# A state-space scan and a maxout FFN: another order of the opening and of the first two blocks, weight fetches moved, last units by token halves

## The chip, the cores and the metric

The kernel runs on one core of one Trainium2 chip. The metric is the device time of one execution in microseconds, the median of the runs shown. The engines are called as in the profile: PE (TensorE matmuls, with PEld for its weight loads), DVE (VectorE), ACT (ScalarE), POOL (GpSimd) and SP (SyncE, which issues nearly all transfers here).

## The reference

Two stages follow each other. The first is a Mamba-2 scan over 4 batches, 8 heads and 768 positions, head width 32, state width 16. The second is a feed-forward layer whose hidden value is the maximum of three products.

```python
# x, a, B, C: (4, 8, 768, 32 | - | 16 | 16)
for c in range(nc):                                  # chunks along the sequence
    cum = np.cumsum(np.log(np.clip(a, 1e-06, 1.0))[:, :, sl], axis=-1)
    L = np.exp(cum[:, :, :, None] - cum[:, :, None, :]) * causal
    M = np.einsum('bhin,bhjn->bhij', Cc, Bc) * L
    y[:, :, sl] = M @ xc + (Cc @ state) * np.exp(cum)[..., None]
    decay_from_j = np.exp(cum[:, :, -1:] - cum)
    state = exp(sum of log a) * state + sum_j(B_j x_j * decay_from_j)
x = y.transpose(0, 2, 1, 3).reshape(3072, 256)
h = np.maximum(np.maximum(x @ w1, x @ w2), x @ w3)   # w1, w2, w3: 256 x 768
out = h @ w_out                                      # 768 x 256
```

## The kernel before, in words

The sequence is cut into six blocks of 128 positions (`NC`), each holding all four batches, so 512 tokens (`BLK`). Within a block the scan works on two halves of 64 positions (`W`). For each block there is the scan, which gives y transposed (`yT`), and the FFN. The FFN uses max(a, b, c) = b + max(a - b, 0, c - b): the weight differences w1 - w2 and w3 - w2 are formed once (`d`, line 881), the maximum is taken over two products and zero, and the product with w2 is folded into the output matrix (`fold`). Block 0 multiplies in plain float32 (line 841 for its first two units, by position halves, line 1251 for the others). The blocks after it split every operand into a high part H, a rest L and a cross term S in the float32r type, and take three faster products, near (H), far (L) and late (S), at lines 926 and 956. The products with the output matrix are at lines 1038 (block 0), 1070 and 1123 (last block).

The program is ordered by hand. Each engine runs its own queue in the order in which the Python code emits instructions, and that order is spelled as words. `OPENING` (line 1260) is the list for block 0 and the preparation of block 1; `FIRST`, `SECOND`, `STEADY` and `LAST` (lines 1276 to 1331) hold one string for each of the twelve up-units of blocks 1, 2, 3 to 4, and 5. A word emits a function's instructions on all engines at once: `R` and `S0`, `S1` form and spread the sums that the decays of block 0 need, `x0` to `x3` are the exponentials (line 418), `tC` and `tB` the transposes by DVE (line 576), `sc0` the scores (line 588), `p0` to `p3` their product with the decays (line 594), `bm`, `Am`, `mid` the state in the middle of the block, `y0` and `y1` the output of its two halves (line 778), `m0` the first FFN products of the first halves (unit pair 0 and 1) and `n0` to `n11` the twelve units of block 0. `z` adds one dummy matmul to the next `warm` call (line 410). `E` is one exponential of the decays of a later block, `X02` and `X24` its products on PE (line 514), which read `left` and `right`: log sums that go out to DRAM (`sums`, line 485) and come back rearranged (lines 491, 497). `q` is one product of block 0 with the output matrix, `bu0:1` one of the eight steps that form and split the differences of one weight pair, `g` turns a part of w2 for the fold, `d` is one down product, `l` one for the last block.

The weights arrive as 64-bit words of which a float32 must be made. `fetch` (line 193) issues one of twelve transfers of 512 KB on SP. `decode` (line 219) takes two steps on ACT and two on DVE, `sign` (line 233) one on DVE (line 237) and one addition on POOL (line 239). Before the word list starts, the kernel loads C and B of block 0, fetches one weight, loads x of block 0 and fetches `NFETCH` = 8 more (lines 259 to 264). SP runs in order: a transfer that waits holds back all transfers behind it. An issue also waits until the transfer eight places before it has landed, by the semaphores of the built program.

For the last block, `last_next` (line 1106) runs the queue of output products: for each term near, far and cross, in the last term by pairs of batches, then scales the sum (ACT) and adds the cross part (DVE, line 1137), and stores.

Of the kernel before, what the change touches and what calls it, by code (L numbers as in the profile page):

```python
# [12 lines left out]
F32R = mybir.dt.float32r  # L13
# [7 lines left out]
def kernel(  # L21
# [46 lines left out]
    NFETCH = 8  # L68
# [140 lines left out]
    def decode_steps():  # L209
# [3 lines left out]
        if rb is None:  # L213
            return (lambda: None), (lambda: None)
# [4 lines left out]
        def first():  # L219
# [6 lines left out]
            nc.scalar.activation(r.bitcast(FP32), lo, AF.Copy, bias=2.0, scale=2.0 ** -51)  # L226
            nc.vector.tensor_scalar(
# [5 lines left out]
        def second():  # L233
# [4 lines left out]
                out=r, in0=hi, scalar=0x80000000, in1=r, op0=ALU.bitwise_and, op1=ALU.bitwise_or)  # L238
            nc.gpsimd.tensor_tensor(  # L239
# [6 lines left out]
    def decode():  # L246

        first, second = decode_steps()
        first()
        unsigned.append(second)  # L250

    def sign():

        unsigned.pop(0)()
# [117 lines left out]
    def by_token(rows, src, name, scale, bank):  # L372
        return scaled(turned(rows, src, name, bank), name, scale)

# [8 lines left out]
    def first_rows():  # L383
# [10 lines left out]
        for u in range(2):  # L394
            nc.vector.tensor_tensor(
# [47 lines left out]
    def first_from_last():  # L443
# [3 lines left out]
            out=both, in0=cum0[:, 0, W - 1:W], in1=cum0[:, 0, P - 1:P], op=ALU.add)  # L447
        held["fj0"] = fj = half([P, 3, W], "fj0")
# [3 lines left out]
    def first_by_token():  # L452
        fj = held["fj0"].rearrange("p n i -> p (n i)")
        tp = only("up")([P, 2, P], "fj0_tp")
        nc.tensor.transpose(out=tp[0:W, 0], in_=fj[:, 0:W], identity=ident)
        nc.tensor.transpose(out=tp[:, 1], in_=fj[:, W:], identity=ident)
        rows = tp.rearrange("p n (b h d) -> p n b d h", b=NB, h=NH)[:, :, :, 0]
# [19 lines left out]
    def sums_first():  # L477
        nc.scalar.copy(out=hl[:, 0], in_=a_sb)
        nc.vector.tensor_tensor(out=rest, in0=a_sb, in1=hl[:, 0], op=ALU.subtract)

    def sums_store():
        nc.scalar.copy(out=hl[:, 1], in_=rest)
        nc.vector.tensor_tensor(out=hl[:, 2], in0=rest, in1=hl[:, 1], op=ALU.subtract)
        for p in range(3):
# [16 lines left out]
    def decay_sums(c, bs):  # L501
        L = Ls[c] if c in Ls else decays(c)
        es = [att_bank([P, NH, W], "e") for _ in bs]
        if c == 1:
            for e in es:
# [30 lines left out]
    def scan_b(c, kind):  # L536
# [3 lines left out]
        transposes(tr, st["B"])  # L540
        st["BT"] = BT = half([HN, NB, P], "BT")
        nc.scalar.copy(out=BT, in_=tr)

# [11 lines left out]
    def scan_c(c):  # L555
# [4 lines left out]
        for g in range(2):  # L560
            nc.scalar.mul(CT[:, :, g], tr, parity[:, g:g + 1])
# [36 lines left out]
    def first_turned_b():  # L598

        tp = att_bank([W, NP, HN], "B_tp")  # L600
# [898 lines left out]
```

## Time and profile before

| what | value |
|---|---|
| median of 3 runs | 257.39 us (256.78 to 257.83) |
| profiled execution, its own time | 255.31 us |
| span of that execution | 253.6 us |
| granted TensorE clock, mean | 0.970 |
| busy: PE, DVE, ACT, POOL | 238.5, 148.2, 132.7, 115.4 us |
| HBM read, written | 14.17 MB, 3.29 MB |

A row of a timeline gives the start in microseconds, the busy time, the engine, the line, the operation, output and inputs, shapes, the number of records, and in brackets the idle time of that engine just before with what ended it. A float32 matmul has two records. The row of a line gives the number of records, then minimum, median and maximum of their duration in ns.

### The profile page before, as it was taken

How to read it: one execution, taken by the hardware profiler on the slowest of the kernel's cores; microseconds unless marked ns; L12 is line 12 of the kernel's file. 1: busy time of each engine (PE TensorE's matmuls, PEld its weight loads, DVE VectorE, ACT ScalarE, POOL GpSimd, SP SyncE). 2: the span in 40 equal slices, each digit the busy share in tenths (PEclk: the TensorE clock that was granted, in tenths of full speed). 3: DMA queues.
4: the chain of work that ended last, by engine and by line, in shares of the span. 5: the costliest groups of instructions: out<-in, count | busy, mean ns of one | idle time of the engine just before them, and what ended most of it. 6: DMA issues, size and time to landing. Idle time of an engine off the chain costs nothing.

```text
span 253.6 us, 7038 instructions
## 1 busy us (share of the span) xinstructions
PE 238.5 (94%) x2992; PEld 188.4 (74%) x2992; DVE 148.2 (58%) x229; ACT 132.7 (52%) x251; POOL 115.4 (46%) x109
## 2 busy tenths in 40 slices
PE   7846969999999999999999999999999999999993
PEld 3335725656676787888888888888888888998992
DVE  5797499676667964388833765527755263334223
ACT  2757275562288536366464654746536274344341
POOL 4022335779349948529572451666324224122230
PEclk9985699999999999999999999999999999999998
DMA  3999779302743802026402280002000020002002
GB/s 80 199 320 386 120 106 114 123 12 60 117 70 76 100 3 89 3 57 111 45 1 91 63 126 3 0 3 85 0 3 0 3 85 3 0 0 87 0 0 84
DMA packets 71083, 17.92 MB, mean 71 GB/s; under 512 B 64492, under 2 KB 67980, under 8 KB 71052
## 3 DMA queue, kind: packets, MB, share of 16 engines
q1 hardware_dynamic: 70604, 17.21, 31.4%
q8 instruction: 23, 0.38, 0.6%
q10 hardware_dynamic: 448, 0.26, 0.3%
q14 instruction: 8, 0.07, 0.1%
HBM read 14.17 MB, written 3.29 MB: 69 GB/s over the span
## 4 chain that ended last, share of the span: by engine, by line
PE 59%; issue 0%; DVEq 0%; DVE 0%
PE up L926 19%; PE o L1070 19%; PE up L956 9%; PE near L1123 3%; PE y L763 2%; PE y L747 2%; PE cross L1123 1%; PE s L726 1%; PE A L692 1%; PE e L514 1%; PE E L660 0%; DVEq L1494 0%; DVE ob L1137 0%; DVEq L1137 0%
## 5 line engine op out<-in xcount | busy, mean ns | idle before, releaser
L977 POOL TENSOR_TENSOR hL<-h,hH 128x512 fp32r<-128x512 f32 x30 | 40.0, 1332 | 80.0 <-ACT hH L976 78.9
L933 ACT ACTIVATE up<-up 128x512 f32<-128x512 f32 x60 | 35.3, 589 | 46.0 <-PE up L926 44.0
L829 DVE SCALAR_TENSOR_TENSOR hS<-hL,hH 128x512 fp32r<-128x512 f32 x30 | 31.2, 1039 | 35.1 <-POOL hL L977 35.0
L926 PE MATMUL up<-yH,wH 128*128 128x512 f32 x120 | 40.8, 421 | 0.2 <-DVE h L965 0.2
L965 DVE SCALAR_TENSOR_TENSOR h<-up,m 128x512 f32<-128x512 f32 x30 | 20.7, 689 | 30.9 <-PE up L956 26.1
L956 PE MATMUL up<-yS,wS 128*128 128x512 f32 x120 | 37.7, 394 | 0.0
L926 PE MATMUL up<-yL,wL 128*128 128x512 f32 x120 | 37.2, 391 | 0.0
L239 POOL TENSOR_TENSOR w<-w_u,w_r 128x512 uint32<-128x512 uint32 x12 | 16.2, 1358 | 33.5 <-DVE w_r L237 33.5
L961 ACT COPY m<-up 128x512 f32<-128x512 f32 x30 | 17.6, 586 | 20.8 <-PE up L956 20.0
L926 PEld LDWEIGHTS up<-yL,wL 128*128 128x128 f32 x120 | 22.5, 188 | 5.2
L956 PEld LDWEIGHTS up<-yS,wS 128*128 128x128 f32 x120 | 21.8, 188 | 6.1 <-ACT up L933 1.5
L528 POOL TENSOR_SCALAR_AFFINE_SELECT L<-L 64x1024 f32<-64x1024 f32 x16 | 19.6, 1228 | 11.0 <-ACT L L523 10.4
L976 ACT ACTIVATE hH<-h 128x512 fp32r<-128x512 f32 x30 | 18.7, 625 | 7.8 <-DVE h L965 7.8
L926 PEld LDWEIGHTS up<-yH,wH 128*128 128x128 f32 x120 | 18.8, 190 | 3.1 <-DVE h L965 1.0
L1251 PE MATMUL up<-yT,d 128*128 128x512 f32 x40 | 19.1, 605 | 0.0
L734 DVE TENSOR_TENSOR L<-s,L 128x512 f32<-128x512 f32 x20 | 13.0, 682 | 5.2 <-PE s L726 5.2
L1070 PE MATMUL o<-wL,hL 128*128 128x256 f32 x96 | 15.7, 285 | 0.0
L1070 PE MATMUL o<-wH,hH 128*128 128x256 f32 x96 | 15.6, 285 | 0.0
L1070 PEld LDWEIGHTS o<-wH,hH 128*128 128x128 f32 x96 | 14.1, 189 | 1.5
L1070 PE MATMUL o<-wS,hS 128*128 128x256 f32 x96 | 14.7, 286 | 0.0
L1070 PEld LDWEIGHTS o<-wS,hS 128*128 128x128 f32 x96 | 13.4, 190 | 1.2 <-issue 0.2
L1070 PEld LDWEIGHTS o<-wL,hL 128*128 128x128 f32 x96 | 13.4, 190 | 0.7 <-issue 0.2
(175 smaller groups left out, 410.8 us busy)
## 6 DMA issues: line engine op xcount, KB each, us to landing
raw_x<-in_x_dram SPq DMA_DIRECT2D x6, 512.0 KB
out_dram<-ob SPq DMA_DIRECT2D x11, 256.0 KB
rb<-in_moe_w_dram SPq DMA_DIRECT2D x5, 512.0 KB
early<-in_moe_w_dram SPq DMA_DIRECT2D x4, 512.0 KB
rb<-in_moe_w_out_dram SPq DMA_DIRECT2D x3, 512.0 KB
raw_B<-in_B_dram SPq DMA_DIRECT2D x5, 256.0 KB
runs_C<-in_C_dram SPq DMA_DIRECT2D x32, 32.0 KB
runs_B<-in_B_dram SPq DMA_DIRECT2D x32, 32.0 KB
```

The costliest lines, as they stand in the source:

```text
L239: nc.gpsimd.tensor_tensor(out=t.rearrange("p k f -> p (k f)").bitcast(U32), in0=u, in1=r, op=ALU.add)
L528: nc.gpsimd.affine_select(out=part, in_=part, pattern=[[0, 2], [0, NH], [1, W]], compare_op=ALU.is_ge, fill=0.0, base=0, channel_multiplie ...
L829: nc.vector.scalar_tensor_tensor(out=out, in0=L, scalar=-RAISE, in1=H, op0=ALU.mult, op1=ALU.add)
L926: nc.tensor.matmul(out=bank, lhsT=up_parts[q, i][z][:, k, g * P:(g + 1) * P], rhs=y_parts[c][z][:, k], start=(z == 0 and k == 0), stop=(z ...
L933: nc.scalar.mul(bank, bank, RAISE + 1.0)
L956: nc.tensor.matmul(out=up, lhsT=up_parts[q, i][2][:, k, g * P:(g + 1) * P], rhs=y_parts[c][2][:, k], start=False, stop=(k == KD - 1), skip ...
L961: nc.scalar.copy(out=m, in_=up)
L965: nc.vector.scalar_tensor_tensor(out=h, in0=up, scalar=0.0, in1=held["m"], op0=ALU.max, op1=ALU.max)
L976: nc.scalar.mul(H, h, NEAR)
L977: nc.gpsimd.tensor_tensor(out=L, in0=h, in1=plain(H), op=ALU.subtract)
L1070: nc.tensor.matmul(out=o[b // 2][:, b % 2], lhsT=left[:, b * P:(b + 1) * P], rhs=right, start=(first and b % 2 == 0), stop=True, skip_grou ...
L1251: nc.tensor.matmul(out=p, lhsT=of(k), rhs=yT[0][:, k], start=(k == 0), stop=(k == KD - 1))
```

## The change

The diff does six things.

1. Words can be split by engine. Functions become generators; where they `yield`, the word stops, and a later word with a plus sign goes on with the rest. So `n0` puts the matmuls into PE's queue and `n0+` the copy into ACT's queue, at a place of its own.
2. `OPENING`, `FIRST` and `SECOND` are written anew in another order. `STEADY` and `LAST` stay. `y0` and `y1` become eight words by batch (`ya0` to `ya3` for the first half, `yc0` to `yc3` for the second); `cols` (an array for the decays of later blocks) is a word of its own.
3. `NFETCH` is 2 instead of 8; the other fetches are words in `OPENING`. In SP's queue of the built program, five fetches stand ahead of the three stores of the sums and five between those and `left`; before, ten stood ahead of the stores.
4. Four more places take dummy matmuls, and there are more `z`: 24 dummies in `warm` instead of 4.
5. a of block 0 is loaded by two transfers instead of four, and POOL sets the tile to 1.0 ahead of them.
6. In the last block, the last two up-units are done by token halves (`token_half`): a unit now takes both differences of the last feature group for 256 tokens, not one difference for 512, and copy, maximum, split and cross term work on halves. The last output products finish batches 0 and 1 before 2 and 3.

```diff
-    NFETCH = 8
+    NFETCH = 2
...
-    for k in range(REP):
-        eng = nc.sync if k % 2 == 0 else nc.scalar
-        eng.dma_start(
-            out=a0[k::REP], in_=a_rows[:, 0:P])
+    nc.gpsimd.memset(a0, 1.0)
+    for k, eng in enumerate((nc.sync, nc.scalar)):
+        eng.dma_start(out=a0[k::REP], in_=a_rows[:, 0:P])
...
             nc.scalar.activation(u.bitcast(FP32), hi.bitcast(FP32), AF.Abs)
             nc.scalar.activation(r.bitcast(FP32), lo, AF.Copy, bias=2.0, scale=2.0 ** -51)
+            yield
             nc.vector.tensor_scalar(
...
+    def token_half(c, u):
+
+        return u - (NU - 2) if c == NC - 1 and u >= NU - 2 else None
+
+    def half_products(bank, c, r, z):
+        q, g = divmod(NF - 1, 2)
+        for i in range(2):
+            for k in range(KD):
+                nc.tensor.matmul(
+                    out=bank[:, i * HB:(i + 1) * HB],
+                    lhsT=up_parts[q, i][z][:, k, g * P:(g + 1) * P],
+                    rhs=y_parts[c][z][:, k, r * HB:(r + 1) * HB],
+                    start=(z == 0 and i == 0 and k == 0), stop=(z > 0 and k == KD - 1),
+                    skip_group_check=True)
...
-        "R em clip S0 z tC E fj0 cp S1 z tB x3 bt0 x1 fetch cm x0 x2 log sc0 p0 bT p3 decode minus1 p1 p2 y0 sign bm run z Am mid "
-        "decode E sign y1 hl1 decode decode bu0:1 g fj LB1 sign hl2 m0 Lx1 bu0:1 E "
-        "n0 sign decode sign "
-        "n1 z "
-        "n2 bt bu1:1 "
-        "n3 rows decode X02 decode sign LC1 decode 1 decode E LB0 sign decode X24 1 "
-        "n4 g q bu1:1 Bd0 sign sign E "
-        "n5 t E q fetch "
-        "n6 decode bu2:1 q c A0 1 "
-        "n7 q sign e sign E 1 1 minus "
-        "n8 bu1:1 s bd fetch bu0:1 "
-        "n9 bu2:1 9 A q 1 1 1 bu0:1 q decode y bu1:1 1 bu0:1 E bu0:1 "
-        "n10 "
-        "n11 v bu0:1 load2 q sign Y q q 9 "
+        "fetch z z z z z em fj0 fj0+ z z z z z bt0 R R+ cols clip tC em+ cm log run tB cp hl1 cp+ hl1+ S1 bt0+ S0 decode decode+ sign x3 sc0 x0 p3 z z bT x1 fetch p0 z z z z ya0 p1 bm x2 ya1 hl2 p2 hl2+ hl2+ z Am mid z yc0 yc2 yc1 minus1 decode decode decode+ sign yc0+ yc1+ yc2+ fetch fetch fetch yc3 yc3+ ya3 ya2 ya3+ sign+ fetch sign+ z z z z z g decode decode decode bu0:1 decode z m0 "
+        "n0 n0+ decode+ sign decode+ sign+ bu0:1 fj bu0:1 "
+        "n1 n1+ sign sign+ "
+        "n2 "
+        "n3 fetch decode+ sign g+ rows X02 E X24 bt LB1 decode+ sign E E sign+ bu1:1 g "
+        "n4 n2+ decode n3+ sign+ q q decode+ sign sign+ q decode+ sign g+ bu1:1 bu1:1 decode decode+ sign q decode LB0 Bd0 n4+ "
+        "n5 n5+ E "
+        "n6 n6+ A0 1 e LC1 t bt+ bo:1 decode+ sign sign+ sign+ bu2:1 t+ t+ c "
+        "n7 sign+ fetch n7+ "
+        "n8 fetch c+ e+ 1 s decode decode+ sign "
+        "n9 decode sign+ q bd Lx1 bu2:1 bu0:1 1 1 1 q 1 A 1 bu0:1 "
+        "n10 minus load2 q q n8+ bu2:1 n9+ n10+ 1 y v v+ decode+ bu0:1 sign sign+ Y 1 1 "
+        "n11 n11+ "
     )
     FIRST = [
-        "Z bu1:1 X04 E",
-        "Z q E bu1:1 bu1:1 bu0:1",
-        "Z load E E t 1 q",
...
+        "Z e 1 bu1:1 load bu1:1 1 bu1:1 bu0:1 bu1:1",
+        "Z q X04 E E E bu0:1",
+        "Z E q q t c 1",
...
     for word in OPENING.split():
+        if word[-1] == "+":
+            go_on(word[:-1])
+            continue
...
-            last += [(t, z, range(NB)) for t in LAST_TERMS[:-1] for z in range(3)]
-            last += [(LAST_TERMS[-1], z, bs) for bs in ((0, 1), (2, 3)) for z in range(2)]
-            last += [(LAST_TERMS[-1], 2, bs) for bs in ((0, 1), (2,), (3,))]
+            two, end = LAST_TERMS[-2:]
+            last += [(t, z, range(NB)) for t in LAST_TERMS[:-2] for z in range(3)]
+            last += [(t, z, (0, 1)) for t in (two, end) for z in range(2)]
+            last += [(t, 2, (0, 1)) for t in (two, end)]
+            last += [(t, z, (2, 3)) for t in (two, end) for z in range(2)]
+            last += [(two, 2, (2, 3)), (end, 2, (2,)), (end, 2, (3,))]
...
+        if r is not None:
+            half_products(up, c, r, 2)
+            m = half([P, HB], "m")
+            nc.scalar.copy(out=m, in_=up[:, 0:HB])
+            cross_next()
+            h = half([P, HB], "h")
+            nc.vector.scalar_tensor_tensor(
+                out=h, in0=up[:, HB:], scalar=0.0, in1=m, op0=ALU.max, op1=ALU.max)
+            held["h"] = c, NF - 1, h, slice(r * HB, (r + 1) * HB)
+            return
...
-    for _ in range(2):
+    while len(last) > 13:
         last_next()
```

More of the change, by code (lines that the diff above doesn't have):

```diff
@@ L1331, with later_from_j, run, go_on @@
     ]
+    def later_from_j():
+        tp = turned(R, held["fj"], "from_js", att_bank)
+        yield
+        from_js = scaled(tp, "from_js", 1.0)
+        for m in range(1, NC):
+            from_j[m] = from_js[:, :, m]
+    begun = {}
+    def run(c, word, steps):
+        if not steps:
+            return
+        if c:
+            for _ in steps:
+                pass
+            return
+        if part(steps):
+            begun.setdefault(word, []).append(steps)
+    def go_on(word):
+        if not part(begun[word][0]):
+            begun[word].pop(0)
+    def part(steps):
+        try:
+            next(steps)
+        except StopIteration:
+            return False
+        return True
     def act(c, word):
@@ L1356, in act @@
         elif word == "bt":
[L1357 to L1359 removed]
+            run(c, word, later_from_j())
         elif word == "bd":
@@ L1395, in act @@
         elif word == "v":
-            scan_own(n, range(NB // 2, NB))
-            nc.scalar.copy(out=seen, in_=blocks[n]["y"][1][:, 0, 0, 0:1])
+            run(c, word, second_own(n))
         elif word == "Y":
```

238 lines of the change are left out of this document (140 added, 98 removed).

## The prediction

> **What bounds the kernel now.** I read the page first (the span, and the granted clock in 40 slices), then the stretches, then each engine's timeline in the stretches where TensorE sits idle or slow.
>
> ```profile
> span 253.6 us, 7038 instructions
> ...
> PEclk9985699999999999999999999999999999999998
> ```
> ```profile
> 0.00:20.00 20.00, 14.33 (x300) 7.82 (x304) 14.56 (x40) 10.31 (x20) 4.33 (x16) 0.92 0.76 206
> 20.00:40.00 20.00, 15.76 (x79) 9.50 (x72) 14.78 (x28) 13.01 (x27) 6.57 (x6) 0.74 0.85 187
> 40.00:60.00 20.00, 20.00 (x280) 12.43 (x285) 15.48 (x23) 11.36 (x20) 14.64 (x13) 1.00 0.35 78
> 100.00:222.00 122.00, 121.99 (x1748) 104.82 (x1747) 66.49 (x91) 64.19 (x122) 55.12 (x49) 1.00 0.18 36
> 222.00:253.60 31.60, 27.20 (x179) 24.66 (x178) 9.66 (x15) 11.95 (x22) 6.90 (x6) 0.98 0.10 34
> ```
>
> The second view gives, for each stretch, its length, then busy time with the number of instructions for PE, PEld, DVE, ACT and POOL, then granted clock, DMA share and GB/s. From 40 us on TensorE has work without a break: 20.00 of 20.00, later 121.99 of 122.00. There the kernel is as long as its matmuls, and the diff leaves their number as it is; a new order of blocks one and two can lose time there but has almost none to win. Time that is not matmul work lies in the first 40 us (5.67 + 4.24 us idle, and a clock of 0.74 in the second stretch) and in the tail (4.40 us). The first 40 us in stretches of three:
>
> ```profile
> 12.00:15.00 3.00, 0.95 (x33) 0.56 (x32) 2.92 (x6) 2.50 (x5) 0.00 (x0) 1.00 0.96 267
> 15.00:18.00 3.00, 1.51 (x64) 1.14 (x64) 3.00 (x8) 1.72 (x3) 1.27 (x1) 0.79 0.93 315
> 24.00:27.00 3.00, 2.69 (x6) 2.19 (x7) 2.80 (x4) 1.02 (x5) 1.26 (x1) 0.50 1.20 302
> 30.00:33.00 3.00, 3.00 (x12) 1.74 (x11) 1.46 (x4) 3.00 (x6) 0.40 (x1) 0.93 0.86 140
> ```
>
> From 12 to 18 us TensorE is busy for 2.46 us of 6, the clock falls to half inside 15-18, and it is back only in 30-33, although TensorE was at 2.69 of 3 from 24 on. DVE is the full engine there (2.92 and 3.00 of 3). What the half clock and the waits cost, on TensorE's timeline:
>
> ```profile
> 24.31 6.71 PE L841 MATMUL up<-yT,d 128*128 128x256 f32 x16 [1.89 <-DVE d L881]
> 31.07 1.88 PE L1251 MATMUL up<-yT,d 128*128 128x512 f32 x4
> 34.70 0.59 PE L506 MATMUL e<-mask,ident 128*128 128x512 bf16 x2
> 37.59 0.41 PE L514 MATMUL e<-right,left 32*64 32x512 bf16 x4 [2.29 <-DMA right<-sums]
> 38.80 1.98 PE L1251 MATMUL up<-yT,d 128*128 128x512 f32 x4
> 92.02 3.62 PE L1051 MATMUL o<-fold,yT 128*128 128x256 f32 x16
> ```
>
> The first FFN products (words m0 and n0) start at 24.31 because the weight difference d came late. They take 6.71 us, where sixteen records of the same shape took 3.62 at 92 us at full clock. Later the decay products wait 2.29 us for `right`, a DMA.
>
> **The change, part by part.** Term A, the start of m0. DVE and POOL rows:
>
> ```profile
> 5.33 0.35 DVE L387 TENSOR_SCALAR factors<-opening,dsel,ndsel 128x128 f32<-128x128 f32 x1
> 11.69 1.29 DVE L594 TENSOR_TENSOR L<-s,L 128x512 f32<-128x512 f32 x2 [1.30 <-ACT L L418]
> 17.69 0.39 DVE L627 TENSOR_TENSOR mid<-A,parity 128x256 f32<-128x256 f32 x1
> 18.00 0.41 DVE L227 TENSOR_SCALAR w_u<-w_u 128x512 f32<-128x512 f32 x1
> 18.79 0.69 DVE L237 SCALAR_TENSOR_TENSOR w_r<-early,w_r 128x512 uint32<-128x512 uint32 x1
> 21.09 0.41 DVE L479 TENSOR_TENSOR sums_rest<-opening,hl 96x256 f32<-96x256 f32 x1
> 23.57 0.68 DVE L881 TENSOR_TENSOR d<-w 128x512 f32<-128x512 f32 x1
> L239 POOL TENSOR_TENSOR w<-w_u,w_r x12: 1262/1274/1719, 15.8 to 65.8; 128x512 uint32<-128x512 uint32 x12
> ```
>
> DVE runs its queue in order. Between the second decode (18.00 to 19.48) and d (23.57) stand the copies of y, sums_rest and two further decodes. In the changed program's order d follows the second decode and two copies directly, and the third and fourth decode come behind it. Walk: `factors` starts at 5.33 now; two DMAs for a in place of four let it start perhaps 0.2 earlier (my choice; a POOL memset that they wait for keeps it from being more), 5.1. From there to `mid` DVE takes 12.36 us (5.33 to 17.69), of which 1.30 is a wait for the first exponentials. The new order pulls sums_rest (0.41) and the third part of hl (0.41 by the same row) ahead of `mid`, and moves the four scans ahead of the second transpose, so the exponentials come while DVE is busy: the 1.30 goes, 0.8 comes. Against that, five dummy matmuls (words z) stand ahead of the word em now:
>
> ```profile
> 2.80 1.91 PE L434 MATMUL spread<-mask,ident 128*128 128x512 bf16 x4
> 5.39 1.08 PE L638 MATMUL E<-opening,to_n 32*32 32x64 f32 x32 [0.68 <-DVE opening L341]
> ```
>
> Five at 0.42 (four in 1.91 with the last one's drain) behind 4.71 end at 6.8, em ends at 7.9 instead of 6.5, and the exponential of E0 (0.4, an estimate from the other small steps) is there at 8.3, where DVE wants it at about 8.0 for Cd: 0.3 lost. `mid` starts at 5.1 + 12.36 - 1.30 + 0.82 + 0.3 = 17.3, the second decode takes 1.48 behind it, with `mid` itself 0.39: 19.1 (the copies of y fit between, TensorE's y being done). POOL adds 1.27: 20.4; d 0.68: 21.1, less some overlap of queue steps, 21.0. A = 24.31 - 21.0 = 3.3. Bounds: 1 (the first exponentials late by the full 1.3 again, and the copies) and 5.
>
> Term B, the clock. The changed program has 24 dummy matmuls (4 before): five ahead of em and five ahead of bt0, seven between the scores and `mid`, five ahead of the base transposes, and two more. Seven at about 0.21 (two in 0.59 above, with one's drain) add 1.5 us in the poor stretch; the scores (1.2, as the later ones quoted under D) move into it with the later transpose, and some y products (0.6, my estimate) leave it: about 4.6 of 6 busy instead of 2.46, 77% against 41%. The only fall in this trace follows the 41%. So m0 and n0 take 3.62: B = 6.71 - 3.62 = 3.1. Bounds 0 and 3.1. The dummies cost 0.3 in A and nothing else, since TensorE waits for DVE at each of those places; if that cover were gone, they would cost their 5 us.
>
> By the Trainium skill (TensorE: Matmul & The Clock Gate, What's actually happening) full clock comes after about one busy window of some 3.4 us; the rows above show 6 us, from 24.31 into the stretch at 30. By its figure a closed gate would cost m0 and n0 only about 1.7 instead of 3.1; the measured rows decide here.
>
> Term C, `right`. The weight fetches are not tied to a request by any semaphore: the built order shows only that fetches six to ten now stand behind the store of the sums in SP's queue instead of ahead of it.
>
> ```profile
> 14.68 2.69 SPq L206 DMA_DIRECT2D rb<-in_moe_w_dram  x4
> 21.05 8.59 SPq L485 DMA_DIRECT2D sums<-hl  x3
> 30.23 3.96 SPq L497 DMA_DIRECT2D left<-sums  x3
> 34.24 1.77 SPq L491 DMA_DIRECT2D right<-sums  x3
> ```
>
> SP sat on the store of the sums until 29.64, since hl was late and everything queued behind it. Now hl is done at 17.2 (just ahead of `mid`); five fetches at 0.67 follow (20.6), left (3.96) and right (1.77): 26.3, and the matmul came 1.6 after the last issue (36.01 to 37.59): 27.9. TensorE wants it after n3: 21.0 + 3.62 + 3.6 (n2, n3 and a small transpose, 31.07 to 34.70) + 0.59 = 28.8. Covered by 0.9; C = 2.3, bounds 0 and 2.3. What is late if hl slips: fetches six to ten themselves, which no longer lie in memory before they are needed.
>
> Term D, what the earlier start runs into: the decoding. TensorE arrives 3.3 + 3.1 + 2.3 = 8.7 us sooner, and DVE must deliver weights sooner. From d at 21.0 to the eleventh weight DVE has nine decodes at 1.48 (13.3), three more d (2.0), and about 4.3 of other work (four h at 0.69, as the row at 244.89 has it, and three small ones of about 0.5): 40.6, with POOL's 1.27, 41.9. TensorE asks for that weight in the words q behind n9:
>
> ```profile
> 53.41 1.21 PE L726 MATMUL s<-CP,BT 32*64 32x128 f32 x64
> 57.25 1.99 PE L1038 MATMUL o<-w,h 128*128 128x256 f32 x8
> L230 DVE TENSOR_SCALAR w_u<-w_u x12: 426/428/1380, 13.5 to 59.0; 128x512 uint32<-128x512 uint32 x12
> L237 DVE SCALAR_TENSOR_TENSOR w_r<-rb,w_r x8: 679/684/1544, 31.8 to 64.9; 128x512 uint32<-128x512 uint32 x8
> ```
>
> n4 starts at 21.0 + 3.62 + 3.6 + 1.8 (the decay words, 34.70 to 38.80, without their stall) = 30.0; six units at 1.8, four q at 1.0 and the scores' 1.2 bring it to 46.0, a little more with the small words. Slack 4.1. But a decode step that meets POOL's add takes up to 1380 instead of 426 ns, 1544 instead of 679: 1.8 us for one decode, 16.3 for nine. The medians (428, 684) lie at the minima, so about half collide at most: 8.1, a stall of 4.0. Between 0 and 4.0 I take D = 2.0, the middle; the far bound, all nine, is 12.2.
>
> Blocks one and two: TensorE's idle time of 40 to 222 us is under a microsecond, so 0, with the transfers for block two still 20 DMAs behind `minus`.
>
> Term E, the tail.
>
> ```profile
> 244.89 0.69 DVE L965 SCALAR_TENSOR_TENSOR h<-up,m 128x512 f32<-128x512 f32 x1 [1.04 <-PE up L956]
> 247.72 0.69 DVE L829 SCALAR_TENSOR_TENSOR hS<-hL,hH 128x512 fp32r<-128x512 f32 x1 [2.13 <-POOL hL L977]
> 248.56 0.65 PE L1123 MATMUL cross<-wS,hS 128*128 128x256 f32 x4
> 249.08 1.35 DVE L1137 TENSOR_TENSOR ob<-raised,cross 128x512 f32<-128x512 f32 x3 [0.67 <-PE cross L1123]
> ```
>
> The chain from h to hS (244.89 to 248.41) is hidden under matmuls that end at 248.56, so halving it shortens nothing by itself; it would matter (3.5 us) if those matmuls were fewer, and both programs have 36 products behind the last `late`. But three additions (1.35) stand behind the last product now, and in the new order two of the four outputs are added some 1.4 us earlier: one addition of about 0.4 remains exposed. E = 0.8, bounds 0 and 1.4.
>
> Sum: 3.3 + 3.1 + 2.3 - 2.0 + 0.8 = 7.5. The profiled execution took 255.31 (span 253.6); 247.8 follows. The runs' median, 257.39, lies 2.08 above it; I carry that over: **249.9 us**.
>
> **The rivals.** The clock closes all the same (for: 77% is my count, and dummies that wait for a bank bunch up; against: five of them stand shortly before m0): B is lost, 253.0.
>
> `right` still lands late (for: the cover is 0.9 and the weights share the queue; against: the store leaves SP 12 us sooner): C is lost, 252.2. With it the words "on request" have done nothing.
>
> DVE runs short (for: 2.92 and 3.00 of 3 busy already, and the same work in 8.7 us less; against: the medians above): with two thirds of nine decodes colliding 10.9, a stall of 6.8, 4.8 more than in D, 254.7.
>
> Slower: every decode from the third on collides with the add of the one before, because the new order sets them back to back. Place: the first q behind n9. Price: 16.3 less the slack of 4.1, 12.2, which is 10.2 more than in D: 260.1. It decides from about eight of the nine on (8 x 1.8 = 14.4, less 4.1 is 10.3, against A + B + C + E = 9.5). For: POOL has nothing else there, so its adds follow each decode at once; against: an add that falls into one of DVE's waits harms nobody, and in 40-60, with POOL busy for 14.64 of 20, DVE's 23 steps kept TensorE full. The Trainium skill (SBUF — State Buffer, Who interferes with whom) says why it could be all: VectorE and GpSimd hold one port pair by an exclusive lock, and the second blocks fully. The trace agrees for single steps (1380 against 426), not for their median.
>
> **How the numbers follow.** Forecast 0.52; clock 0.13 (253.0); `right` late 0.06 (252.2); DVE short 0.11 (254.7); better, with D at zero, 0.05 (247.9); gains and stalls cancel 0.05 (about 257.4); all collide 0.08 (260.1). A run of this kernel can be told from no change by about 0.5%, 1.3 us: faster 0.52 + 0.13 + 0.06 + 0.11 + 0.05 = 0.87, same 0.05, slower 0.08. The forecast's own range, by A and D, is 247.5 to 252; to hold 8 in 10 it reaches to the clock and DVE cases, 246.5 to 254.5.
>
> **What would show it.** Right: m0 at about 21 us, its sixteen records in about 3.6, PEclk without a 5 or 6 after the start, no wait of the decay products for `right`, DVE's last addition under 0.5 us long in the tail, and TensorE idle for some 2 us between 40 and 60 in waits for POOL's w. Wrong: a clock of 0.5 at m0 (B), PE idle for more than 4 us behind n4 with the releaser w or w_r (D), or new idle time in blocks one and two.

## The result and the profile after

The changed kernel takes 246.17 us (median of 6 runs, 245.22 to 246.39), the kernel before on the same chip 257.23 (256.78 to 258.17). The ratio is 0.956, with a 95% interval of 0.953 to 0.958. The forecast was 249.9 with a range of 246.5 to 254.5, so the direction was right and the time lies 0.3 under the range. The profiled execution of the changed kernel took 246.31; profile against profile the gain is 9.0 us, median against median 11.1. The sum had promised 7.5 between profiles. Medians and ratios leave out the few runs that lie more than 1.5% above the fastest run of the same kernel.

The page of the changed kernel, its span and the granted clock:

```profile
span 244.6 us, 7115 instructions
...
PEclk9889999999999999999999999999999999999999
```

Its stretches (length, then busy time of PE, PEld, DVE, ACT, POOL, then granted clock, DMA share, GB/s):

```profile
0.00:20.00 20.00, 16.83 (x341) 9.11 (x342) 15.16 (x45) 13.27 (x26) 5.83 (x18) 0.91 0.83 229
20.00:40.00 20.00, 19.20 (x80) 11.37 (x79) 18.93 (x27) 15.30 (x31) 10.72 (x8) 1.00 1.04 227
40.00:60.00 20.00, 19.75 (x405) 12.82 (x404) 13.77 (x25) 8.77 (x17) 14.07 (x14) 1.00 0.14 30
60.00:80.00 20.00, 18.88 (x152) 14.52 (x151) 16.72 (x20) 12.54 (x23) 14.21 (x12) 1.00 0.75 109
100.00:222.00 122.00, 121.66 (x1576) 104.75 (x1575) 66.13 (x94) 64.30 (x120) 49.98 (x43) 1.00 0.17 33
```

From 20 to 40 us TensorE is busy for 19.20 of 20 us at full clock, where it had 15.76 at 0.74. The half clock is not gone (the two 8 in the row of slices), but it is over by 14 us. New is the idle time of 1.12 us in 60 to 80. TensorE's timeline, the places of the prediction's terms in order:

```profile
10.21 2.45 PE L601 MATMUL s<-CP,BT 32*64 32x128 f32 x64 [1.78 <-ACT CP L676]
...
20.77 0.67 PE L877 MATMUL up<-yT,d 128*128 128x256 f32 x2
22.16 3.18 PE L877 MATMUL up<-yT,d 128*128 128x256 f32 x14 [0.73 <-issue]
25.18 3.60 PE L1325 MATMUL up<-yT,d 128*128 128x512 f32 x8
...
29.14 0.41 PE L522 MATMUL e<-right,left 32*64 32x512 bf16 x4
...
48.21 1.89 PE L1108 MATMUL o<-w,h 128*128 128x256 f32 x8
...
72.80 0.73 PE L981 MATMUL up<-yH,wH 128*128 128x512 f32 x2 [1.12 <-DVE h L1031]
```

m0 starts at 20.77 instead of 24.31 (A: 3.54). From its start to n2, that is for m0 and n0 together, it takes 4.41 instead of 6.76 (B: 2.35), and 0.73 of that is a wait with the releaser "issue", which no semaphore ends. The products with `right` have no wait (C: 2.29). The products behind n9, at 48.21, have none either (D). SP shows why `right` came in time:

```profile
13.68 2.87 SPq L492 DMA_DIRECT2D sums<-hl  x3
...
17.10 2.63 SPq L205 DMA_DIRECT2D rb<-in_moe_w_dram  x4
19.83 2.56 SPq L504 DMA_DIRECT2D left<-sums  x3
22.49 2.35 SPq L498 DMA_DIRECT2D right<-sums  x3
```

The store of the sums leaves SP by 16.6, where it was 29.64, and `right` is asked for at 22.49 instead of 34.24. In the tail the last products end at 241.07, 3.53 us ahead of the span's end, against 249.21 and 4.39 before (E: 0.86):

```profile
240.43 0.64 PE L1193 MATMUL cross<-wS,hS 128*128 128x256 f32 x4
241.06 0.75 DVE L1209 TENSOR_TENSOR ob<-raised,cross 128x256 f32<-128x256 f32 x2 [0.54 <-ACT raised L1205]
```

### The profile page after: what moved, and what is told of

Read it like the earlier page. It is cut to its first block, busy times and chain, and to the rows that moved or that the text cites. A ratio compares the mean times of both kernels' runs of the same rounds, so it can differ in the third digit from the quotient of the medians.

```text
span 244.6 us, 7115 instructions
## 1 busy us (share of the span) xinstructions
PE 235.1 (96%) x3024; PEld 186.6 (76%) x3024; DVE 145.5 (59%) x231; ACT 134.2 (55%) x254; POOL 115.4 (47%) x111
## 4 chain that ended last, share of the span: by engine, by line
PE 90%; DVE 4%; issue 2%; DMA 1%; ACT 1%; SPq 1%; DVEq 0%; POOL 0%; POOLq 0%
PE up L981 22%; PE o L1140 19%; PE up L1022 11%; PE up L1325 7%; PE y L790 3%; PE o L1108 3%; PE near L1193 3%; PE y L769 3%; PE fold L1081 2%; PE s L748 2%; PE A L714 2%; PE up L877 2%; PE o L1121 1%; PE cross L1193 1%; PE up L966 1%
## 5 line engine op out<-in xcount | busy, mean ns | idle before, releaser
L1044 POOL TENSOR_TENSOR hL<-h,hH 128x512 fp32r<-128x512 f32 (+1 forms) x31 | 39.4, 1272 | 80.9 <-ACT hH L1043 79.7
L865 DVE SCALAR_TENSOR_TENSOR hS<-hL,hH 128x512 fp32r<-128x512 f32 (+1 forms) x31 | 28.6, 921 | 31.1 <-POOL hL L1044 31.1
L981 PE MATMUL up<-yH,wH 128*128 128x512 f32 x116 | 39.5, 422 | 1.1 <-DVE h L1031 1.1
L1031 DVE SCALAR_TENSOR_TENSOR h<-up,m 128x512 f32<-128x512 f32 x29 | 20.0, 689 | 30.2 <-PE up L1022 28.1
L1022 PE MATMUL up<-yS,wS 128*128 128x512 f32 x116 | 36.6, 396 | 0.0
L981 PE MATMUL up<-yL,wL 128*128 128x512 f32 x116 | 36.0, 391 | 0.0
L1027 ACT COPY m<-up 128x512 f32<-128x512 f32 x29 | 17.0, 586 | 18.9 <-PE up L1022 17.1
L981 PEld LDWEIGHTS up<-yL,wL 128*128 128x128 f32 x116 | 21.8, 188 | 5.0
L536 POOL TENSOR_SCALAR_AFFINE_SELECT L<-L 64x1024 f32<-64x1024 f32 x16 | 19.8, 1235 | 6.7 <-ACT L L531 6.1
L1043 ACT ACTIVATE hH<-h 128x512 fp32r<-128x512 f32 (+1 forms) x31 | 19.0, 611 | 6.4 <-DVE h L1031 4.6
L981 PEld LDWEIGHTS up<-yH,wH 128*128 128x128 f32 x116 | 18.0, 190 | 4.0 <-issue 1.4
L1325 PE MATMUL up<-yT,d 128*128 128x512 f32 x40 | 18.6, 600 | 0.0
```

The source lines that it names most:

```text
L536: nc.gpsimd.affine_select(out=part, in_=part, pattern=[[0, 2], [0, NH], [1, W]], compare_op=ALU.is_ge, fill=0.0, base=0, channel_multiplie ...
L865: nc.vector.scalar_tensor_tensor(out=out, in0=L, scalar=-RAISE, in1=H, op0=ALU.mult, op1=ALU.add)
L981: nc.tensor.matmul(out=bank, lhsT=up_parts[q, i][z][:, k, g * P:(g + 1) * P], rhs=y_parts[c][z][:, k], start=(z == 0 and k == 0), stop=(z ...
L1022: nc.tensor.matmul(out=up, lhsT=up_parts[q, i][2][:, k, g * P:(g + 1) * P], rhs=y_parts[c][2][:, k], start=False, stop=(k == KD - 1), skip ...
L1027: nc.scalar.copy(out=m, in_=up)
L1031: nc.vector.scalar_tensor_tensor(out=h, in0=up, scalar=0.0, in1=held["m"], op0=ALU.max, op1=ALU.max)
```

## The experiments

Ratios are to the kernel before on the same chip and carry 95% intervals. The kernel before is not the same on every chip (medians 254.5 to 257.2), the changed kernel nearly is: 246.17 above, and 246.07 and 245.30 below. The variants e1 to e4 ran on a chip on which the changed kernel was not timed; they are set against its times elsewhere.

> The changed kernel itself, beside its variants on the same chip: 246.2 us (245.2 to 246.4 before), and its profile with TensorE's first FFN products cut in two by a gap of 0.5 to 0.8 us that no semaphore ends.

246.07 us (245.41 to 246.43), with a gap of 1.18 instead of 0.5 to 0.8. On a third chip, where 246.1 was expected, it took 245.30 (five runs), with a gap of 1.64.

### Why profile and median of the kernel before differ

The prediction added 2.08 us for the distance between the profiled execution (255.31) and the median (257.39). Two more profiles were taken of the kernel before, without an edit.

> The kernel before, unchanged, for a second profile: which of its two kinds of run the first profile was. Theory G: its runs differ by one more window at half clock (mean granted clock 0.97 against 0.963, about 2 us), which follows from the wait for `right`: in a profile with 0.965 or less, PEclk falls a second time between 35 and 42 us, and the products right behind that wait are slow (0.64 us where 0.41 was, n4 over 2.5 us where 1.98 was); in a profile of 0.968 or more it doesn't. Rival H: the two kinds differ elsewhere (in the tail, or in blocks one to five).

> The same once more, since either kind can come: by G each profile of 0.965 or less shows the second fall, each of 0.968 or more doesn't.

Both came with a mean clock of 0.963 (256.50 and 256.95 us; the first profile had 0.970). The page, the timeline and a window of the first of them:

```profile
PEclk9955897999999999999999999999999999999998
```
```profile
37.11 0.41 PE L514 MATMUL e<-right,left 32*64 32x512 bf16 x4 [3.42 <-DMA right<-sums]
37.45 0.69 PE L506 MATMUL e<-mask,ident 128*128 128x512 bf16 x2
38.06 0.64 PE L514 MATMUL e<-right,left 32*64 32x512 bf16 x4
38.63 3.27 PE L1251 MATMUL up<-yT,d 128*128 128x512 f32 x4
```
```profile
38.00:40.00 2.00, 2.00 (x7) 0.97 (x7) 1.95 (x5) 1.29 (x3) 0.27 (x1) 0.50 1.05 98
```

The "7" in the seventh slice is a second closing of the clock. It follows the wait for `right`, which is 3.42 us here and was 2.29 in the first profile; behind it four records of n4 take 3.27 instead of 1.98. The second new profile shows the same (wait 3.39, n4 3.46). The wait is longer there because the first half clock ended sooner: m0 and n0 take 5.56 and 5.76 us instead of 6.71, while `right` comes at about the same time (37.11 and 37.40 against 37.59). m0, n0 and the wait together are 9.00, 8.98 and 9.15 us in the three profiles, so a faster m0 alone is no gain in this kernel.

Of 65 executions of the kernel before on five chips, 40 had a mean clock of 0.968 or more, with a median of 255.03 us, and 25 had 0.962 to 0.965, with a median of 256.81; on one chip the two lie 0.8 to 2.4 apart. The clocks of the first batch are not on record, but all six of its runs (256.78 and more) lie above the slowest of the 40 (256.31), to which the profile with its 0.970 belongs. So the 2.08 is mostly one more window at half clock, it follows from the wait for `right`, and it went with that wait. The clocks of the changed kernel's six first runs are 0.990 to 1.0.

The Trainium skill (TensorE: Matmul & The Clock Gate, What's actually happening) calls the window free-running, so that the same kernel can have a different number of slow matmuls from run to run. The traces agree: the changed kernel has half clock from 10.65 to 14.05 us in its first profile and none before 243 us in its third. The length of a wait does not decide alone: the kernel before kept the clock after 2.29 us and lost it after 3.39 and 3.42, but in e2 below the profiled execution lost it after 2.08.

### A and C alone and together, in the kernel before

```diff
 e5  -y1 hl1 decode decode bu0:1 g          +y1 bu0:1 hl1 decode decode g
 e11 -Am mid ... y1 hl1 ... sign hl2 m0     +Am mid hl1 hl2 ... y1 ... sign m0
 e6  both: Am mid hl1 hl2 ... y1 bu0:1 decode decode g ... sign m0
 e14 e6, and the loads LB1 and Lx1 moved from ahead of `rows` to behind it
```

> The kernel before with one step moved: the first weight difference d stands on VectorE directly behind the second decode and the two copies of y, ahead of the sums' rest and of decodes three and four (the order of the changed kernel; nothing else). Theory P (the terms A and C end at the same place): m0 starts 1.9 us earlier, at 22.4, where TensorE's own earlier work ends, but `right` depends on the sums, which come no earlier, so the wait for `right` grows from 2.3 to about 4.2 to 4.9 and the time is within 1 us of the kernel before. Rival S (the terms add up): 1.9 us faster than before.

257.02 us, ratio 1.007 (1.004 to 1.010): slower. m0 starts at 21.85 instead of 24.31, and all of it goes into the wait for `right`, which the longer wait then answers with the half clock:

```profile
37.06 0.64 PE L514 MATMUL e<-right,left 32*64 32x512 bf16 x4 [5.95 <-DMA right<-sums]
...
39.17 3.21 PE L1251 MATMUL up<-yT,d 128*128 128x512 f32 x4
```

The wait grew to more than the 4.9 expected, since the clock also came back earlier in m0 and n0 (4.98 us for both instead of 6.71). The rival falls: the terms do not add up one at a time.

> The kernel before with the two steps that split and store the sums moved from behind decodes three and four to directly behind `mid`; d and the fetches as before. Theory P: the store leaves SP some 4 to 5 us sooner, the wait of 2.3 us for `right` is gone, and the steps (0.8 us of VectorE and their waits for ScalarE) start m0 about 1 us later: 0.8 to 1.5 us faster than before. Rival F: the five fetches ahead of the store keep the queue and the DMA engines full, so that `right` lands as late as before: not faster, or slower by the 1 us of m0.

254.26 us, ratio 0.996 (0.993 to 0.999): 1.0 faster, as theory P had it, but by another way than it said. The wait for `right` is still 1.16 us, and 11 of 12 executions have a mean clock of 0.970 to 0.972, against 16 of 26 with 0.968 or more in the kernel before on this chip. Those 16 have a median of 254.95, these 11 one of 254.23, so about half of the gain, as an estimate, is that the second closing became rare.

> The kernel before with both steps moved: sums split and stored behind `mid`, and d ahead of decodes three and four; no dummies, the fetches ahead as before, blocks one and two and the tail as before. Theory P: both waits go, m0 about 1 us earlier than before and no wait for `right`: 3 to 3.5 us faster than before, more than the two alone together, and the rest of the 9 us between the kernels is the clock, the small products ahead of m0 and the tail. Rival S (terms add up): the sum of the two runs alone.

254.68 us, ratio 0.997 (0.993 to 1.0005), not told apart from the kernel before. Theory P falls: 0.8 instead of 3 to 3.5. Rival S falls too: 1.8 lost and 1.0 gained would be 0.8 slower. SP's timeline and TensorE's show where it went:

```profile
22.59 6.04 SPq L145 DMA_DIRECT2D raw_x<-in_x_dram  x1
28.75 3.75 SPq L497 DMA_DIRECT2D left<-sums  x3
32.55 1.78 SPq L491 DMA_DIRECT2D right<-sums  x3
```
```profile
35.83 0.64 PE L514 MATMUL e<-right,left 32*64 32x512 bf16 x4 [3.41 <-DMA right<-sums]
```

The sums had left SP by 20.3, but the load of raw_x held SP for 6.04 us with `left` and `right` behind it. Hence e14.

> As the run with both steps moved in the kernel before, and besides `left` and `right` are asked for right behind the store of the sums: the loads of raw_B and raw_x, of which the second held SP for 6.0 us with `left` and `right` queued behind it, follow them. Theory Q: what kept C from being gained there was SP's queue; now the wait for `right` is under 0.5 us, the clock doesn't fall a second time, and the time is 3 us or more under the kernel before. Rival F: the transfers themselves are late behind 2.5 MB of weights (the fetches still stand ahead of the store), the wait for `right` stays over 2 us, and the time is that of the run with both steps moved, about 1 us under the kernel before.

253.53 us, ratio 0.990 (0.987 to 0.994), 2.5 faster by the ratio. The wait for `right` is 0.79 instead of under 0.5, and seven of eight executions have a clock of 0.973 to 0.980. The clock does not fall a second time. So theory Q is right that the two loads stood in the way, but not that they were all: `left` is asked for at 27.96, only 0.8 sooner than in e6, since SP now waits for the store itself to land, which left SP by 21.44 with ten fetches ahead of it. That is what rival F says. In the changed kernel, with five fetches ahead, SP asks for `left` at 19.83 without such a wait. The rows of SP's waits (total, times, longest) and of TensorE, where the next things are late:

```profile
SPq L497 <- DMA sums<-hl: 6.5, 1, 6.5
```
```profile
33.08 0.41 PE L514 MATMUL e<-right,left 32*64 32x512 bf16 x4 [0.79 <-DMA right<-sums]
...
37.35 1.13 PE L1038 MATMUL o<-w,h 128*128 128x256 f32 x4 [0.64 <-POOL w L239]
```

The wait for a decoded weight is new, and TensorE waits another 0.95 us for the load of raw_C, which now stands behind. That keeps the time short of the 3 us expected. The remaining 7.4 us to the changed kernel lie in the clock, in the rest of its order and in the tail; they were not taken apart further by runs.

### C in the changed kernel: the fetches ahead again

```diff
-    NFETCH = 2
+    NFETCH = 8
     (the first six words `fetch` of OPENING taken out)
```

> The changed kernel with eight more weights fetched ahead of the word list again (NFETCH 8, the first six words fetch taken out), so that nine fetches stand ahead of the store of the sums in SP's queue. Theory P: the store and the way back of left and right come later, the decay products X02 wait for right again, and up to 2.3 us are lost, about 248.4. Rival F: what made right late before was that hl came late, and hl is early now; SP's store still comes after at most one fetch more of waiting, the weights arrive sooner, and the time stays within 0.5 us of 246.2.

247.51 us (three runs: 247.51, 247.51 and the profiled 249.61), ratio 0.968 (0.962 to 0.975). That is 1.4 over the changed kernel by the medians and 2.2 by the means of the runs. `left` is asked for at 26.00 instead of 19.83, since SP waits 5.5 us for the store to land, and the wait is back, with half clock behind it in the profiled run; the other two kept a clock of 1.0:

```profile
SPq L504 <- DMA sums<-hl: 5.5, 1, 5.5
```
```profile
31.75 0.41 PE L522 MATMUL e<-right,left 32*64 32x512 bf16 x4 [2.08 <-DMA right<-sums]
32.09 1.04 PE L514 MATMUL e<-mask,ident 128*128 128x512 bf16 x2
33.05 0.64 PE L522 MATMUL e<-right,left 32*64 32x512 bf16 x4
```

Rival F falls: hl is early here and `right` is late all the same. Requests behind the store are worth 2.08 us of waiting in the trace and 1.4 us or more in the time, and what they spare is the store's way through the weights ahead of it.

### B: the dummies, and the gap in m0

```diff
-z z z z z            (each place of them in OPENING)
+
```

> The changed kernel without its 24 dummy matmuls (the words z are taken out of the opening). Theory P, as forecast: the dummies keep the half clock away from m0 and n0. Without them the clock that fell at 10.65 us in the changed kernel's profile stays at 0.5 when m0 starts, m0 and n0 take 6 to 7 us instead of 4.4, and the time is 2.3 to 3 us above the changed kernel, about 248.5 to 249. Rival O: the new order alone keeps TensorE full enough; m0 starts at about 20.8 with the full clock, and the time is within 0.5 us of 246.2, or below it, since em comes earlier.

246.04 us, ratio 0.959 (0.954 to 0.964). The time is rival O's, but not its reason: the clock is at half from 9.55 us on, though TensorE is busy for 4.79 of 6 us from 12 to 18, and comes back only at 23.2, among the products of m0 and n0:

```profile
PEclk9756999999999999999999999999999999999999
```
```profile
12.00:18.00 6.00, 4.79 (x133) 3.28 (x125) 5.10 (x11) 5.00 (x9) 1.27 (x1) 0.50 0.98 345
```
```profile
21.04 4.69 PE L877 MATMUL up<-yT,d 128*128 128x256 f32 x16
25.56 3.60 PE L1325 MATMUL up<-yT,d 128*128 128x512 f32 x8
```

n2 starts at 25.56 against 25.18 with the dummies. They bring the clock back before m0 (at 14.05), but little comes of it: m0 starts at 20.77 instead of 21.04, and at full clock it runs into the gap of 0.73 us. What the gap is was asked next:

```diff
         ys = held["yc"]
-        first_own(1, b, lambda p, n, t: ys[b][p:p + n, t])
         yield
```

> Leaves out 64 small matrix products of block zero's second half (its own tokens' part of y, four groups of 16), so the output lacks that part; with them go 64 weight loads, 128 TensorE instructions ahead of m0. Theory I: the gap after the first two records of m0 is TensorE waiting for its instructions, which the run of small products before it uses up faster than they are fetched (159 instructions in the microsecond from 18 to 19): with 128 fewer the gap is gone and m0 takes 3.6 to 3.7 us from start to end. Rival W: the gap is weights or data held up by the full DMA traffic of that time, which stays: the gap stays at 0.5 us or more. Time: 0.7 to 1.7 under the changed kernel by I, 0 to 1 by W.

The gap is gone, and m0 and n0 run through:

```profile
20.07 3.69 PE L876 MATMUL up<-yT,d 128*128 128x256 f32 x16
```

The time is 245.64 us (ratio 0.963, 0.958 to 0.968), 0.4 under the changed kernel on this chip: less than theory I's 0.7, and within rival W's 0 to 1. And the gap is gone in the run of e9 below as well (m0 at 20.27, 3.71 us for m0 and n0), which leaves no product out, so this run does not decide. More is told by the trace's list of DMA packets. In 19.7 to 19.8 us of the changed kernel's profile it has one packet of 16 KB in an instruction queue:

```profile
q8 instruction: 1, 0.02, 59.5%
```

The products go on at 22.16, about 2.4 us later. The interval is 2.2 to 2.5 us in every profile of these kernels with a gap of half a microsecond or more (packet, go-on): 20.3 and 22.68 in a second profile of the changed kernel, 19.6 and 22.04 in a third (gaps of 1.18 and 1.64), 20.2 and 22.62 in e2, 18.6 and 20.97 in e3, 18.5 and 20.99 in e4, 18.7 and 21.02 in e13, 19.0 and 21.27 in its second profile, 21.5 and 24.00 in its third; in e8, with a gap of 0.21, it is 2.6. In e9 and e10 the packet came at 18.4 and 18.1, so that its 2.4 us were over by 20.8, when TensorE had its first two records done: no gap. The likely reading is that TensorE waits for instructions there, which the small products (85 matmuls and 74 weight loads in the microsecond from 18 to 19) use up quickly. It is not shown: no run moved the packet alone, what sets its time was not tried, and the profile does not say whose instructions it brings.

```profile
18.00:19.00 1.00, 1.00 (x85) 0.91 (x74) 0.97 (x3) 0.49 (x2) 0.37 (x1) 1.00 1.18 368
```

### D: how much room the decodes have

```diff
-            nc.vector.tensor_scalar(out=u..., op0=ALU.max, op1=ALU.min)
+            for _ in range(4 if len(to_done) == 10 else 1):
+                nc.vector.tensor_scalar(out=u..., op0=ALU.max, op1=ALU.min)
+            to_done.append(0)
```

> The eleventh decode takes 1.27 us longer on VectorE (its clip, which gives the same values again, is done four times). Theory P: the changed kernel's decodes are in time by no more than 0.46 us (that weight is there at 47.75 and used at 48.21), so about 0.8 us come on top of the changed kernel, as a wait of the products behind n9 for POOL's w. Rival R: VectorE is not what sets the end here and has spare time until 60 us: within 0.3 of the changed kernel.

The wait is there, 1.05 us:

```profile
48.28 1.99 PE L1111 MATMUL o<-w,h 128*128 128x256 f32 x8 [1.05 <-POOL w L243]
```

In e8, whose n2 starts within 0.2 us of it, the same products start at 47.12 without a wait. POOL's add starts 1.57 later than there (46.96 against 45.39), less a room of 0.46 is 1.1. The median, 246.16 (ratio 0.966, 0.961 to 0.971), does not show it beside the changed kernel's 246.07: opening and tail vary by as much from run to run. Theory P holds in the trace; its time is not told apart.

### E: the tail

```diff
 e4  token_half() returns None                  (no halves, the new order of last products)
 e3  the same, and the old order of last products
```

> The changed kernel with the last up-units over 512 tokens as before, but the new order of the last output products (batches 0 and 1 first). Theory P: the chain h, hH, hL, hS of 3.5 us now has only about 2.1 us of products in front of its first reader, TensorE waits about 1 us in the tail, and the gain of the order is given back: 246.9 to 247.3. Rival: the order of the last products is all of it, halves or not: 246.2, with no wait of TensorE before its last products.

247.5 us (245.98 to 248.8), ratio 0.965 (0.960 to 0.970), by which it is not told apart from the changed kernel (0.956 to 0.964). TensorE waits inside its last products for a split that comes late, as theory P says:

```profile
238.94 0.51 PE L1193 MATMUL near<-wL,hL 128*128 128x256 f32 x2 [0.79 <-POOL hL L1044]
```

> The changed kernel with the old tail: last up-units by difference over 512 tokens, last products in the old order (the scaling of batches 2 and 3 stays in two steps). Theory P: 0.9 us are lost, by the span from the end of the last product to the end (4.4 before, 3.5 changed): 247.0. Rival: the tail's end is set by the last transfer alone; nothing changes, 246.2.

246.19 us (245.69 to 248.74), ratio 0.963 (0.957 to 0.969). No loss in the median, but its profile has a luckier opening (m0 at 19.75, the clock never closed before the tail), and the tail itself is the old one: the last products end 4.5 us ahead of the end instead of 3.53, with three additions behind them.

```profile
239.54 1.35 DVE L1209 TENSOR_TENSOR ob<-raised,cross 128x512 f32<-128x512 f32 x3 [0.66 <-PE cross L1193]
```

The tail's 1.0 is in the trace; the time of this run is inconclusive.

### A version that beats both

The wait of 1.12 us at 72 comes from VectorE's order in block one. The h that TensorE needs stands behind a split of a down weight, which takes 1.62 us instead of 0.68 beside POOL:

```profile
70.52 1.62 DVE L897 SCALAR_TENSOR_TENSOR wL<-wH,w 128x512 fp32r<-128x512 f32 x1
72.06 0.68 DVE L1031 SCALAR_TENSOR_TENSOR h<-up,m 128x512 f32<-128x512 f32 x1
```
```diff
 e8   -"Z q bo:1 bo:1", "Z bu1:1 s 1 1 1",     +"Z q bo:1", "Z bu1:1 s 1 1 1 bo:1",
 e13  the same lines                           +"Z q", "Z bu1:1 s 1 1 1 bo:1 bo:1",
```

> One change in block one's order: of the two splits of the down weights (VectorE, 0.68 and 0.94 us) that stand behind unit 3, one moves behind unit 4. Theory P: TensorE's wait of 1.12 us at 72.8 us in the changed kernel's profile exists because VectorE's h of that unit is queued behind these splits; with one of them later the wait is gone and nothing else waits: 245.1, that is 1.1 under the changed kernel. Rival R: block one is short of VectorE time as a whole, the wait turns up again at the next h or at the next split weight: within 0.4 of the changed kernel.

246.16 us, ratio 0.965 (0.961 to 0.970): nothing gained, the wait is still 1.11. This tests neither theory: the word that was moved is the step on POOL, and VectorE's order is unchanged.

> The changed kernel with both split steps of a down weight in block one moved from behind unit 3 to behind unit 4: the one on VectorE (1.62 us beside a step of GpSimd) no longer stands ahead of the h that TensorE waits 1.1 us for at 72. Theory P: that wait is gone and the time is 1.0 us under the changed kernel, 245.1. Rival R: VectorE is the full engine of this stretch, the wait comes back at the next h, within 0.4 of the changed kernel's 246.1.

244.54 us, ratio 0.959 (0.956 to 0.963). VectorE's h starts right behind hS, the wait is gone, and none comes in its place:

```profile
69.68 0.68 DVE L1031 SCALAR_TENSOR_TENSOR h<-up,m 128x512 f32<-128x512 f32 x1
```
```profile
60.00:80.00 20.00, 20.00 (x155) 15.88 (x154) 15.35 (x18) 12.45 (x24) 16.69 (x12) 1.00 0.75 108
```

Twice more on other chips it took 244.87 (244.5 expected) and 243.96 us. In the last of these the changed kernel ran on the same chip:

> The version with the two split steps behind unit 4, beside the changed kernel: 244.6 us, 1.0 to 1.6 under it.

243.96 (ratio 0.954, 0.949 to 0.959) against 245.30 (0.960, 0.955 to 0.966): 1.3 us less in the median. The intervals against the kernel before overlap, but set against each other the two are told apart: each of the six runs (243.35 to 244.43) lies under each of the five (244.46 to 246.97).

## Why the prediction was off

**The offset (failed).** "The runs' median, 257.39, lies 2.08 above it; I carry that over." This is the larger part of the 3.7 us between 249.9 and 246.2. The 2.08 was not an overhead that both kernels share. It is a second window at half clock behind the wait for `right`, in many executions of the kernel before, and the prediction's own term C removes that wait. Without it the forecast is 247.8. The rest lies between the profiles, 9.0 us instead of 7.5: D did not come, and B fell 0.8 short.

**D (failed).** "Between 0 and 4.0 I take D = 2.0, the middle." It measured 0; TensorE's idle time from 40 to 60 is 0.25 us. The collisions came (four decode steps of 1.37 to 1.39, two of 1.48 and 1.54 and one of 0.80 us in the changed kernel, about 6 us more than without, against 8.1 assumed). But TensorE reached the words behind n9 at 48.21, not at 46.0: n4 came 1.3 us later than computed, with the gap in m0, and the words behind it took 0.9 longer. And VectorE was not full: ahead of the eleventh weight it waited 0.99 and 0.49 us for TensorE's products. That is why the room is again 0.46 us in e8, where TensorE comes at 47.12. In e10, where it comes at 46.87, it is 0.21, so the wait was not far off, as e9 shows too.

**B (too large, and not for the reason given).** 2.35 instead of 3.1. The clock did close, behind a stretch in which TensorE waited 1.78 us for ACT, and it was open again long before m0. In the 3.41 us ahead of the closing at 10.6 TensorE was busy for 0.48 of the time:

```profile
8.00:10.00 2.00, 0.43 (x9) 0.00 (x0) 2.00 (x7) 1.45 (x3) 0.00 (x0) 1.00 1.06 306
10.00:12.00 2.00, 1.75 (x52) 1.56 (x59) 1.73 (x7) 2.00 (x5) 0.00 (x0) 0.65 1.46 216
12.00:14.00 2.00, 2.00 (x31) 1.07 (x19) 1.41 (x3) 2.00 (x5) 1.27 (x1) 0.50 0.87 271
```

The prediction took 77% of busy time from 12 to 18 as enough to keep the clock. It fell ahead of that stretch, and in e1 80% of busy time there (4.79 of 6 us) did not bring it back. The dummies do bring it back before m0. But without them m0 and n0 take 4.69 us, not 6.71, since the clock returns at 23.2, so against the 3.7 of e9 and e10 they are worth 1.0 us and not 3.1; the 0.73 of "issue" inside m0, which was not foreseen, takes most of that. The 6.71 was itself the longest of three profiles of the kernel before.

**A, C and E (right in size).** m0 at 20.77 (21.0 predicted), no wait for `right`, 0.86 in the tail (0.8). But C's reason was read wrongly in part: "SP sat on the store of the sums until 29.64, since hl was late". The first of the three store requests began at 21.05, right behind its part of hl, and took 7.60 us; the last part of hl was done at 26.48, 2.2 us before that request ended:

```profile
21.05 7.60 SPq L485 DMA_DIRECT2D sums<-hl  x1
25.05 1.43 DVE L483 TENSOR_TENSOR hl<-sums_rest,hl 96x256 bf16<-96x256 f32 x1 [0.20 <-ACT hl L482]
```

So C needs more than the early sums. e11 and e6 stored them early and left the wait at 1.2 to 3.4 us, because ten fetches stood ahead of the store and other loads between it and `right` (e14, e2). The cover was thin, too: in e4, where n2 starts 1.2 us sooner, TensorE waits 0.56 us for `left`. And A without C is a loss (e5). The terms were added as if independent. They are a chain in which the last one decides, so the sum holds only for all together.

**Blocks one and two (failed by 1 us).** Set to 0; idle time from 60 to 80 rose from 0.18 to 1.12, from 40 to 222 from 0.75 to 1.96. e13 shows that it was to be had by order alone.

Between the profiles: A 3.54, B 2.35, C 2.29 and E 0.86 are 9.0, as measured; the new idle time in blocks one and two is made up by about as much shorter work that I have not placed.

## What to carry to other kernels

Before adding a profile's distance from the median to a forecast, ask what the runs differ in: the mean granted clock of each run tells, and here the change that removed a wait of TensorE removed the extra half-clock window behind it too. Gains in front of one join (a start, a clock, a transfer) do not add up one by one; price them together, look in the issuing queue for what stands between a store and the load that depends on it, and for what stands ahead of the store, since the load waits until the store has landed. And check that a word moves an instruction on the engine that is late.

## What was not expected of the hardware

TensorE seems to wait for its own instructions: gaps of 0.5 to 2.5 us behind a dense run of small matmuls (159 instructions in a microsecond) end 2.2 to 2.5 us after a 16 KB packet of an instruction queue, in nine profiles. The half clock comes in whole windows: its 17 stretches ahead of the tail, in twelve profiles, last 3.41, 6.83, 10.24 or 13.66 us, which are one to four times 3.41. In the 3.41 us ahead of each of them TensorE was busy for 0.49 of the time at most; of the windows near them that kept the clock, all were busy for 0.59 or more but one, with 0.44, which is the one with the wait of 2.29 us in the first profile of the kernel before. So where a wait falls among these windows counts as well as its length. And a small store is late behind large loads: 144 KB of sums, gone from SP by 21.44 us with ten fetches of 512 KB ahead, landed 6.5 us later (e14); with five ahead, in the changed kernel, SP asked for what depends on it 3.3 us later without a wait.
